# A recurrence and two layers on one core: interleaved half products, swapped rows, later conversions, and one subtraction on VectorE

## The chip, the cores and the metric

The kernel runs on one core of a Trainium2 chip. The metric is device time in microseconds (us), the median of several executions. The engines are called by the profile's names: PE (TensorE's products, PEld its weight loads), DVE (VectorE), ACT (ScalarE), POOL (GpSimd) and SP (SyncE, which issues most loads).

## The reference, cut to what matters

```python
for t in range(S):                                   # B=4, H=8, S=768, D=40
    y[:, :, t] = einsum('bhd,bhde->bhe', r_t, state)
    Sa = einsum('bhde,bhe->bhd', state, a_t)
    state = state * w_t[..., None] - einsum('bhd,bhe->bhde', Sa, b_t)
    state = state + einsum('bhd,bhe->bhde', v_t, k_t)
x = y as 3072 tokens x 320
h = x @ w_in;  x = max(h, 0)**2 @ w_out              # layer 1: 320 -> 2048 -> 320
h = x @ w_in2; out = (h - tanh(h)) @ w_out2          # layer 2
```

## The kernel before, in words

**The recurrence** is computed in six segments of 128 time steps. Two passes k cover a segment (16 of the 32 batch-heads each), so there are twelve passes, and a pass works on two halves j of eight heads. Scans on DVE (L192, L196) form the products of the decays, `front` and `keys` turn the scaled inputs on PE, `solve` inverts small triangular matrices on DVE for two passes at a time, and `back` walks through the segment in four chunks c of 32 steps. For each chunk and each half `back` multiplies the state zi by the scaled a (pu, L399, eight products of 104 rows, 32 weight columns, 40 streamed columns), ACT copies the result into rows of vu (L401), PE multiplies the keys kbn by vu (pd, L423, eight products), and DVE adds that to the state (zi, L428, two additions). In every second chunk the state is also turned (pz, L393). Half j of a chunk writes rows 64 c2 + 32 to 64 c2 + 63 of its vu, with c2 = c mod 2. `result` forms the outputs y from vu, kbn and a masked matrix (pm, am, py) and stores them for layer 1.

**The two layers** work on twelve tiles of 256 tokens each. A tile of a layer is eight steps m of 256 hidden columns: 16 products hp (L789; the fp32 values are carried as a high part xh and a low part xl), the activation, which gives gh and gl, and 12 products acc (L738) of gh and gl with the second weights wo. In layer 1 ACT makes gh and POOL makes gl (L817); the eight blocks of the second weights are loaded from DRAM anew for each tile. In layer 2 ACT runs four activations (L857 to L860), DVE forms h - tanh h (L863, and L864, L847, L848 for small h), ACT rounds it to gh (L852), and POOL subtracts gh from it (gl, L853). Ahead of each tile POOL splits its input into xh and xl (L710, L713, L714).

**The weights** arrive as 64-bit floats and are converted on the chip, piece by piece: a raw load on SP, an ACT operation, four DVE operations (L578 to L581), an ACT operation that gives the high part and a POOL subtraction for the low part (L585). Layer 1's first weights are 12 pieces of 512 columns that stay in SBUF. Its second weights are 16 pieces of 320 columns that go to DRAM, all of them before layer 1 begins. Layer 2's weights follow during layer 1, in batches of 14 pieces with a pause in front of the next solve.

**The order.** The code is written as threads (back, fronts, scalings, result, conversions, layer 1), which a planner's clock weaves together; a thread yields the time at which it may go on, and a scheduler then places the instructions of each engine by priority: `back` highest, conversions and layer 1 lowest. Each engine runs its own list in order. In the names of the rows a number behind an underscore is a buffer: zi_170 and zi_171 are the two halves' states, vu_176 and vu_177 their vu, kbn_162 and kbn_163 their keys.

## Time and profile before

| | us |
|---|---|
| median of 3 runs (lowest, highest) | 1394.27 (1388.3, 1395.91) |
| profiled execution, its own time | 1393.79 |
| its span, first to last instruction | 1391.6 |
| PE busy | 1221.7 |
| DVE busy | 947.2 |
| ACT busy | 830.0 |
| POOL busy | 675.2 |

The mean granted TensorE clock of the profiled execution is 0.941 of full speed. Layer 1's products run beside the recurrence from about 190 to 957 us; layer 2's weights are loaded after that, and layer 2's products run from about 1010 us to the end. A time of a line is the time that its engine was busy with it; it bears on the end only where the chain of waits passes through it.

### The profile page before, as it was taken

The numbers are of one execution on the slowest core, as the hardware profiler recorded it, in microseconds if no ns is written. First come the engines' busy times: TensorE is split into PE (matmuls) and PEld (weight loads), VectorE is DVE, ScalarE is ACT, GpSimd is POOL, SyncE is SP. The second block draws the span as 40 slices with busy tenths as digits, with TensorE's granted clock in tenths as the row PEclk, the third lists the DMA queues.
The fourth block names the chain that finished last, engine by engine and source line by source line (L and its number), as shares of the span: only waits on it lengthen the run. The fifth ranks groups of instructions, "written<-read, shape, count | busy, mean of one in ns | idle before, by whom it ended". The sixth has DMA issues, their size and how long they took to land.

```text
span 1391.6 us, 40716 instructions
## 1 busy us (share of the span) xinstructions
PE 1221.7 (88%) x16682; PEld 1136.5 (82%) x16682; DVE 947.2 (68%) x1812; ACT 830.0 (60%) x1768; POOL 675.2 (49%) x713
## 2 busy tenths in 40 slices
PE   1347778999799988999799999999899999999996
PEld 1246668888789877888788889999899999999995
DVE  7899785555854675356935671321269999999996
ACT  4364627574466736574465746544477777777785
POOL 5366534445444635245533643245555555555543
PEclk9986868989999988999999999999999999999999
DMA  6444544554545535454554534236920000000000
GB/s 159 114 122 143 157 150 136 154 171 137 163 138 164 170 103 161 133 157 132 160 159 134 159 103 147 85 110 217 391 72 19 24 31 22 22 22 22 22 11 22
DMA packets 94406, 164.12 MB, mean 118 GB/s; under 512 B 17696, under 2 KB 66272, under 8 KB 94212
## 3 DMA queue, kind: packets, MB, share of 16 engines
q1 hardware_dynamic: 65028, 124.02, 29.8%
q0 software_dynamic: 9600, 21.68, 5.1%
q10 hardware_dynamic: 19584, 15.74, 3.4%
q8 instruction: 134, 2.20, 0.7%
q14 instruction: 60, 0.49, 0.1%
HBM read 133.81 MB, written 27.53 MB: 116 GB/s over the span
## 4 chain that ended last, share of the span: by engine, by line
DVE 35%; PE 32%; issue 11%; ACT 10%; DMA 8%; POOL 4%; ACTq 0%; SPq 0%; POOLq 0%; DVEq 0%
DVE e L847 10%; PE hp L789 8%; PE acc L738 7%; DVE e L863 4%; DVE e L864 4%; PE pu L399 3%; DVE wx L192 3%; DMA raw<-in_moe_w_in_dram 2%; PE pd L423 2%; PE pm L451 2%; DVE inw L196 2%; PE pa L375 2%; ACT tbd L369 2%; DMA raw<-in_moe_w_out_dram 2%; DVE T L313 1%
## 5 line engine op out<-in xcount | busy, mean ns | idle before, releaser
L853 POOL TENSOR_TENSOR gl<-e,gh 128x512 fp32r<-128x512 f32 x96 | 144.3, 1504 | 180.5 <-ACT gh L852 178.3
L817 POOL TENSOR_TENSOR gl<-g,gh 128x512 fp32r<-128x512 f32 x96 | 127.0, 1323 | 177.4 <-ACT g L816 172.2
L789 PE MATMUL hp<-xh,wi 128*128 128x256 f32 x960 | 195.5, 299 | 12.3 <-ACT r L814 9.9
L789 PE MATMUL hp<-xh,wi2s 128*128 128x256 f32 x960 | 170.0, 278 | 1.7 <-DMA wi2s<-wi 1.7
L789 PEld LDWEIGHTS hp<-xh,wi 128*128 128x128 f32 x960 | 155.7, 202 | 15.7 <-ACT r L814 10.9
L847 DVE SCALAR_TENSOR_TENSOR e<-e,e 128x512 f32<-128x512 f32 x96 | 155.9, 1624 | 3.3
L738 PE MATMUL acc<-wo,gh 128*128 128x320 f32 x768 | 147.2, 327 | 3.1 <-DMA wo<-wo 2.8
L789 PEld LDWEIGHTS hp<-xh,wi2s 128*128 128x128 f32 x960 | 141.9, 188 | 1.9 <-DMA wi2s<-wi 1.9
L789 PE MATMUL hp<-xl,wi 128*128 128x256 f32 x576 | 134.9, 298 | 0.0
L738 PEld LDWEIGHTS acc<-wo,gh 128*128 128x128 f32 x768 | 121.5, 199 | 5.5 <-ACT gh L852 3.0
L428 DVE TENSOR_TENSOR zi<-pd,zi 40x160 f32<-40x160 f32 x192 | 61.8, 322 | 90.4 <-PE pd L423 86.0
L789 PE MATMUL hp<-xl,wi2s 128*128 128x256 f32 x576 | 120.7, 278 | 0.0
L852 ACT ACTIVATE gh<-e 128x512 fp32r<-128x512 f32 x96 | 60.8, 633 | 88.6 <-DVE e L848 86.4
L585 POOL TENSOR_TENSOR st<-hc,st 128x160 fp32r<-128x160 f32 (+3 forms) x72 | 51.6, 717 | 112.7 <-ACT st L584 82.3
L789 PEld LDWEIGHTS hp<-xl,wi 128*128 128x128 f32 x576 | 103.2, 203 | 0.7
L863 DVE TENSOR_TENSOR e<-hp,e 128x512 f32<-128x512 f32 x96 | 65.0, 677 | 54.4 <-ACT e L858 48.9
L476 POOL DMA_DIRECT2D yT<-yt x96 | 65.2, 682 | 71.9 <-DVE yt L475 69.7
L814 ACT ACTIVATE r<-hp 128x512 f32<-128x512 f32 x96 | 57.3, 597 | 66.7 <-PE hp L789 65.0
L789 PEld LDWEIGHTS hp<-xl,wi2s 128*128 128x128 f32 x576 | 94.5, 188 | 0.0
L578 DVE TENSOR_SCALAR hc<-hc 128x160 f32<-128x160 f32 (+3 forms) x78 | 29.2, 375 | 94.9 <-ACT hc L569 87.1
L848 DVE COPY_PREDICATED e<-e,e 128x512 f32<-128x512 int32 x96 | 89.6, 933 | 3.2
L399 PE MATMUL pu<-zi,au 104*32 104x40 f32 x1536 | 79.0, 209 | 11.1 <-DVE zi L428 8.4
(154 smaller groups left out, 3151.4 us busy)
## 6 DMA issues: line engine op xcount, KB each, us to landing
wo<-wo SPq DMA_DIRECT2D x96, 640.0 KB
inq<-in_wakb_dram SPq DMA_DIRECT2D x36, 240.0 KB
raw<-in_moe_w_in_dram SPq DMA_DIRECT2D x24, 256.0 KB
raw<-in_moe_w_out_dram SPq DMA_DIRECT2D x16, 320.0 KB
wo<-st ACTq DMA_DIRECT2D x32, 160.0 KB
wi<-st ACTq DMA_DIRECT2D x40, 128.0 KB
raw<-in_moe_w_out_dram SPq DMA_DIRECT2D x32, 160.0 KB
wo<-st ACTq DMA_DIRECT2D x64, 80.0 KB
```

Of the source, the lines that this page charges most:

```text
L399: nc.tensor.matmul(pu[r0:r0 + 32, h, :], lhsT=au[0:104, 4 * (h % 2) + h // 2, 32 * c:32 * c + 32], rhs=zi[0:104, h % 2, h // 2, :], start= ...
L428: nc.vector.tensor_tensor(out=zn, in0=pd[rows], in1=zi[rows, c2, par], op=ALU.add)
L476: getattr(nc, Q_Y).dma_start(out=self.yT[k].rearrange("(a r d) (b t) -> b r d a t", a=4, r=2, b=2)[j, par][:, :, t], in_=yt[rows])
L738: nc.tensor.matmul(acc[n][j], lhsT=g[:, i, 128 * j:128 * j + 128], rhs=w[:, p, i, :], start=(m == 0 and i == 0 and e == 0), stop=(m == 7 a ...
L789: nc.tensor.matmul(hp[:, h, :], lhsT=wt, rhs=xx, start=(e == 0), stop=(e == 7))
L814: nc.scalar.activation(out=r, in_=hp, func=ACTF.Relu)
L817: nc.gpsimd.tensor_tensor(out=gl, in0=g, in1=gh.bitcast(F32), op=ALU.subtract)
L847: nc.vector.scalar_tensor_tensor(out=u, in0=q, scalar=rest, in1=u, op0=ALU.add, op1=ALU.mult)
L848: nc.vector.copy_predicated(out=d, mask=v.bitcast(I32), data=u)
L852: nc.scalar.activation(out=gh, in_=d, func=ACTF.Copy)
L853: nc.gpsimd.tensor_tensor(out=gl, in0=d, in1=gh.bitcast(F32), op=ALU.subtract)
L863: nc.vector.tensor_tensor(out=d, in0=hp, in1=th, op=ALU.subtract)
```

## The change

Five things change.

1. In `back` both halves' pu products stand in turn, in one result tile: half 0 of the first product, half 1 of the first, half 0 of the second, and so on. Half 1 uses the other 64 rows than half 0 (64 (c2 xor j) + 32).
2. The pd products of both halves stand in turn too, in the code.
3. For half 1 the 64-row halves of vu and of the keys are swapped: vn is loaded into the swapped rows, the mask of am has a swapped second copy, and in `keys` each of the four transposes of half 1 becomes two products with the identity, of 64 weight columns each.
4. Before layer 1 only the first eight of the 16 pieces of its second weights are converted (steps 0 to 3). The other half is converted as 16 pieces of 160 columns after layer 1 has begun, before layer 2's weights, and layer 1's first tile waits with each step m from 4 on until its block is due by the planner's clock.
5. In layer 2 the subtraction that gives gl moves from POOL to DVE.

```diff
-C_LM, C_AM, C_ZERO, C_ID = 0, 32, 96, 224
+C_LM, C_AM, C_ZERO, C_ID = 0, 32, 160, 288
...
+F_W, P3, L_W1 = 4, 3, 6
...
+    c[:, C_AM + 64:C_AM + 128] = np.roll(c[:, C_AM:C_AM + 64], 64, axis=0)
...
-                nc.tensor.transpose(pt[:, pr, :], kbf[0:P, pr, blk, :], self.id[0:P, 0:P])
+                if j:
+                    for c in (0, 64):
+                        nc.tensor.matmul(pt[64 - c:128 - c, pr, :], lhsT=kbf[0:P, pr, blk, c:c + 64], rhs=self.id[0:P, 0:P], start=True, stop=True)
+                else:
+                    nc.tensor.transpose(pt[:, pr, :], kbf[0:P, pr, blk, :], self.id[0:P, 0:P])
...
-                (getattr(nc, Q_B) if k else nc.sync).dma_start(out=self.vu[j][64 * c2:64 * c2 + 32, :, :, :, 0:40], in_=vn[s, q, c2])
+                (getattr(nc, Q_B) if k else nc.sync).dma_start(out=self.vu[j][64 * (c2 ^ j):64 * (c2 ^ j) + 32, :, :, :, 0:40], in_=vn[s, q, c2])
...
-            for j in range(2):
-                q = 2 * (k % 2) + j
-                zi, vu, zt, au = self.zi[q][:, c2], self.vu[j], self.zt[j], aus[j]
-                if c2 == 0:
+            zis = [self.zi[2 * (k % 2) + j][:, c2] for j in range(2)]
+            if c2 == 0:
+                pzs = []
+                for zi in zis:
...
-                r0 = 64 * c2 + 32
-                pu = self.ps.tile([128, 8, 40], F32, tag="a", name="pu")
-                for h in range(8):
-                    nc.tensor.matmul(pu[r0:r0 + 32, h, :], lhsT=au[0:104, 4 * (h % 2) + h // 2, 32 * c:32 * c + 32],
-                                     rhs=zi[0:104, h % 2, h // 2, :], start=True, stop=True, tile_position=(0, r0))
-                nc.scalar.activation(out=vu[r0:r0 + 32, blk].rearrange("p a r d -> p (a r) d")[:, :, 0:40], in_=pu[r0:r0 + 32],
+            pu = self.ps.tile([128, 8, 40], F32, tag="a", name="pu")
+            r0 = [64 * (c2 ^ j) + 32 for j in range(2)]
+            for h in range(8):
+                for j in range(2):
+                    nc.tensor.matmul(pu[r0[j]:r0[j] + 32, h, :], lhsT=aus[j][0:104, 4 * (h % 2) + h // 2, 32 * c:32 * c + 32],
+                                     rhs=zis[j][0:104, h % 2, h // 2, :], start=True, stop=True, tile_position=(0, r0[j]))
+            clk.run(0.4)
+            for j in range(2):
+                q, vu, zt = 2 * (k % 2) + j, self.vu[j], self.zt[j]
+                nc.scalar.activation(out=vu[r0[j]:r0[j] + 32, blk].rearrange("p a r d -> p (a r) d")[:, :, 0:40], in_=pu[r0[j]:r0[j] + 32],
                                      func=ACTF.Copy, scale=-1.0)
...
+            pds = [self.ps.tile([128, 4, 40], F32, tag="a", name="pd") for _ in range(2)]
+            for pr in range(4):
+                for j, par in ((0, 0), (1, 1), (0, 1), (1, 0)):
+                    k0, hh = 64 * (c2 ^ j), 4 * par + pr
+                    nc.tensor.matmul(pds[j][64 * par:64 * par + 40, pr, :], lhsT=self.kbn[2 * (k % 2) + j][k0:k0 + 64, blk, 40 * hh:40 * hh + 40],
+                                     rhs=self.vu[j][k0:k0 + 64, blk, pr, par, 0:40], start=True, stop=True)
+            clk.run(0.5)
...
-                k0 = 64 * c2
-                pd = self.ps.tile([128, 4, 40], F32, tag="a", name="pd")
-                for pr in range(4):
-                    for par in range(2):
-                        hh = 4 * par + pr
-                        nc.tensor.matmul(pd[64 * par:64 * par + 40, pr, :], lhsT=kbn[k0:k0 + 64, blk, 40 * hh:40 * hh + 40],
-                                         rhs=vu[k0:k0 + 64, blk, pr, par, 0:40], start=True, stop=True)
...
-                                    in1=cst[:, None, C_AM:C_AM + 64].to_broadcast([128, 8, 64]), op=ALU.mult)
+                                    in1=cst[:, None, C_AM + 64 * j:C_AM + 64 * j + 64].to_broadcast([128, 8, 64]), op=ALU.mult)
...
+                yield lambda: la.wait(m)
                 w, wi = la.wo(m), la.wi(m)
...
-        nc.gpsimd.tensor_tensor(out=gl, in0=d, in1=gh.bitcast(F32), op=ALU.subtract)
+        nc.vector.tensor_tensor(out=gl, in0=d, in1=gh.bitcast(F32), op=ALU.subtract)
...
-        conv1 = cv.run([*cv.w_in(w_in1, lambda j, cols: (chunks(wi1, j, cols), lambda: None), N1), *cv.w_out(w_out1, put_out(cp1, wo1_d, N2, 2), N2)], AHEAD)
+        conv1 = cv.run([*cv.w_in(w_in1, lambda j, cols: (chunks(wi1, j, cols), lambda: None), N1), *list(cv.w_out(w_out1, put_out(cp1, wo1_d, N2, 2), N2))[:2 * F_W]], AHEAD)
+
+        wo_ready = [0] * F_W + [inf] * (8 - F_W)
...
             yield lambda: started[0]
+
+            cv = Convert(tc, l1.cp, (), nc.gpsimd, getattr(nc, Q_LD1))
+            for i, _ in enumerate(cv.run(list(cv.w_out(w_out1, put_out(l1.cp, wo1_d, DM // 2, 1), DM // 2))[4 * F_W:], 0)):
+                if i % 4 == 3:
+                    wo_ready[F_W + i // 4] = clk.t + L_W1
+                yield clk.t + P3
```

PE's list in the second pass, chunk c = 2 (pz, pu, pd of both halves; pm belongs to another pass's results), before:

```order
L393 MATMUL pz<-idt,zi_170 40x40 x8
L399 MATMUL pu<-zi_170,au 32x40 x8
L393 MATMUL pz<-idt,zi_171 40x40 x8
L399 MATMUL pu<-zi_171,au 32x40 x8
L451 MATMUL pm<-rt_178,vut 128x128 x4
L451 MATMUL pm<-rt_179,vut 128x128 x4
L423 MATMUL pd<-vu_176,kbn_162 40x40 x8
L423 MATMUL pd<-vu_177,kbn_163 40x40 x8
```

and after the change (the lines' numbers have moved: pz is L400, pu L408, pd L433):

```order
L400 MATMUL pz<-idt,zi_170 40x40 x8
L400 MATMUL pz<-idt,zi_171 40x40 x8
L408 MATMUL pu<-zi_170,au 32x40
L408 MATMUL pu<-zi_171,au 32x40
L408 MATMUL pu<-zi_170,au 32x40
L408 MATMUL pu<-zi_171,au 32x40
L408 MATMUL pu<-zi_170,au 32x40
L408 MATMUL pu<-zi_171,au 32x40
```

Eight pu of a half stood in a row; now each pu is followed by the other half's, and both pz stand ahead of them.

PE's list of the same pass, chunk c = 1 (pt of L269 are the keys' transposes, pl and pt other parts of the fronts), before:

```order
L399 MATMUL pu<-zi_170,au 32x40 x8
L250 MATMUL pl<-inq 32x64 x3
L399 MATMUL pu<-zi_171,au 32x40 x8
L250 MATMUL pl<-inq 32x64 x6
L269 MATMUL pt<-idt,inqx 128x104 x4
L250 MATMUL pl<-inq 32x64 x3
L269 MATMUL pt<-idt,inqx 128x104 x8
L423 MATMUL pd<-vu_176,kbn_162 40x40 x8
L423 MATMUL pd<-vu_177,kbn_163 40x40 x8
```

and after the change (L275 are half 0's transposes, L273 half 1's products), in the same pass one chunk earlier:

```order
L408 MATMUL pu<-zi_170,au 32x40
L408 MATMUL pu<-zi_171,au 32x40
L275 MATMUL pt<-idt,inqx 128x104 x8
L273 MATMUL pt<-idt,inqx 64x104 x8
L433 MATMUL pd<-vu_176,kbn_162 40x40 x8
L433 MATMUL pd<-vu_177,kbn_163 40x40 x8
L273 MATMUL pt<-idt,inqx 64x104 x8
```

The pd of half 0 still stand eight in a row ahead of those of half 1 here, although the code writes them in turn. Over the whole list of 768 pd, 377 follow one of the other half, 283 one of the same half and 108 another line; of 768 pu, 697 follow one of the other half and none one of the same half.

DVE's list in layer 2's middle, two steps m (e are the five buffers of the activation), before:

```order
L863 TENSOR_TENSOR e_15314<-hp_15291,e_15311 128x512
L864 TENSOR_TENSOR e_15310<-e_15310,e_15311 128x512
L847 SCALAR_TENSOR_TENSOR e_15310<-e_15313,e_15310 128x512
L848 COPY_PREDICATED e_15314<-e_15312,e_15310 128x512
L863 TENSOR_TENSOR e_15360<-hp_15337,e_15357 128x512
L864 TENSOR_TENSOR e_15356<-e_15356,e_15357 128x512
L847 SCALAR_TENSOR_TENSOR e_15356<-e_15359,e_15356 128x512
L848 COPY_PREDICATED e_15360<-e_15358,e_15356 128x512
```

and after the change (L877, L878, L861, L862 are the old L863, L864, L847, L848; L867 is gl, the old L853):

```order
L877 TENSOR_TENSOR e_15474<-hp_15451,e_15471 128x512
L878 TENSOR_TENSOR e_15470<-e_15470,e_15471 128x512
L867 TENSOR_TENSOR gl<-e_15428,gh 128x512
L861 SCALAR_TENSOR_TENSOR e_15470<-e_15473,e_15470 128x512
L862 COPY_PREDICATED e_15474<-e_15472,e_15470 128x512
L877 TENSOR_TENSOR e_15520<-hp_15497,e_15517 128x512
L878 TENSOR_TENSOR e_15516<-e_15516,e_15517 128x512
L867 TENSOR_TENSOR gl<-e_15474,gh 128x512
L861 SCALAR_TENSOR_TENSOR e_15516<-e_15519,e_15516 128x512
L862 COPY_PREDICATED e_15520<-e_15518,e_15516 128x512
```

The gl of a step stands between the next step's L878 and L861, two operations behind the L862 that completes its input.

## Rows read from the trace of the kernel before

**Rows 1.** Engines by stretch: us, busy (instructions) each, clock, DMA share, GB/s.
```profile
100.00:186.00 86.00, 66.26 (x1314) 56.33 (x1312) 71.43 (x158) 47.37 (x117) 49.32 (x51) 0.70 0.49 149
1040.00:1380.00 340.00, 332.43 (x2481) 323.20 (x2479) 328.72 (x352) 255.70 (x461) 174.42 (x118) 1.00 0.07 22
```

**Rows 2.** Output copies L878: ns min/median/max, first and last start.
```profile
L878 ACT ACTIVATE o<-accb x12: 417/424/429, 1052.5 to 1359.4; 128x320 f32<-128x320 f32 x12
```

**Rows 3.** Timeline, tile in layer 2: start, us, operation [idle <-releaser].
```profile
1172.16 1.52 POOL L853 TENSOR_TENSOR gl<-e,gh 128x512 fp32r<-128x512 f32 x1 [2.15 <-ACT gh L852]
...
1172.56 1.67 DVE L847 SCALAR_TENSOR_TENSOR e<-e,e 128x512 f32<-128x512 f32 x1
...
1174.26 0.76 DVE L848 COPY_PREDICATED e<-e,e 128x512 f32<-128x512 int32 x1
```

**Rows 4.** Timeline, layer 2's first tile, DVE and POOL.
```profile
1057.59 0.69 DVE L847 SCALAR_TENSOR_TENSOR e<-e,e 128x512 f32<-128x512 f32 x1
...
1058.32 0.78 DVE L848 COPY_PREDICATED e<-e,e 128x512 f32<-128x512 int32 x1
...
1058.98 0.67 DVE L863 TENSOR_TENSOR e<-hp,e 128x512 f32<-128x512 f32 x1
...
1059.58 0.68 DVE L864 TENSOR_TENSOR e<-e,e 128x512 f32<-128x512 f32 x1
...
1059.90 1.52 POOL L853 TENSOR_TENSOR gl<-e,gh 128x512 fp32r<-128x512 f32 x1 [2.91 <-ACT gh L852]
```

**Rows 5.** Groups, 1030 to 1380: busy us, mean ns, idle before.
```profile
L847 DVE SCALAR_TENSOR_TENSOR e<-e,e 128x512 f32<-128x512 f32 x90 | 145.6, 1618 | 3.1
...
L713 POOL TENSOR_TENSOR xl<-xraw,xh 128x512 fp32r<-128x512 f32 x10 | 17.3, 1729 | 0.1
L714 POOL TENSOR_TENSOR xl<-xraw,xh 64x256 fp32r<-64x256 f32 x10 | 12.2, 1219 | 0.0
L710 POOL CAST xh<-xraw 128x768 fp32r<-128x768 f32 x9 | 11.6, 1286 | 0.0
```

**Rows 6.** Timeline of PE in layer 2, 1147 to 1151 us.
```profile
1147.29 0.63 PE L789 MATMUL hp<-xh,wi2s 128*128 128x256 f32 x4
...
1150.96 0.28 PE L789 MATMUL hp<-xh,wi2s 128*128 128x256 f32 x1
```

**Rows 7.** Chain by line, 850 to 957 us, then 620 to 850.
```profile
by line: PE hp L789 24.0%; PE acc L738 21.4%; PE pu L399 10.7%; PE pm L451 7.6%; PE pd L423 7.4%; PE pa L375 6.6%; PE py L469 4.4%; PE pvt L443 4.2%; PE py L472 3.5%; PE pz L393 3.3%; PE pw L345 2.1%; PE pt L832 1.4%; POOL gl L817 1.2%; PE 
...
by line: issue 12.8%; PE hp L789 11.1%; PE acc L738 11.0%; PE pu L399 4.4%; DVE wx L192 4.3%; DVE inw L196 4.1%; PE pd L423 2.7%; DMA raw<-in_moe_w_out_dram 2.5%; POOL gl L817 2.5%; DVE T L313 2.5%; PE pm L451 2.1%; ACT tbd L369 2.1%; DVE t
```

**Rows 8.** Timeline of POOL at the end of the conversions before layer 1.
```profile
182.56 0.98 POOL L585 TENSOR_TENSOR st<-hc,st 128x320 fp32r<-128x320 f32 x1 [1.24 <-DMA zi<-in_vz_dram]
```

**Rows 9.** Chain of waits by line, 100 to 192 us.
```profile
by line: issue 12.7%; DVE hc L580 6.8%; PE pu L399 6.4%; DMA raw<-in_moe_w_out_dram 5.6%; PE pa L375 5.6%; ACT tbd L369 5.5%; DVE zi L428 5.1%; DVE hc L581 5.0%; DMA xraw<-yT 4.3%; DVE hc L579 3.8%; DVE hc L578 3.6%; ACTq L903 2.6%; ACT st 
```

**Rows 10.** Pieces of the chain, 394 to 442: start, us, records.
```profile
399.17 0.44 PE pz L393 x16
...
400.09 0.69 PE pu L399 x16
...
412.48 0.74 PE pd L423 x32
...
414.75 0.89 PE pm L451 x8
...
426.89 1.26 PE pu L399 x32
```

**Rows 11.** VectorE busy (x instructions) with L581 alone, by stretch.
```profile
186.00:298.00 112.00, 5.10 (x12) 0.83 0.49 147
298.00:370.00 72.00, 3.06 (x2) 0.95 0.57 164
```

**Rows 12.** Groups, whole span: busy us, mean ns, idle <-releaser.
```profile
L428 DVE TENSOR_TENSOR zi<-pd,zi 40x160 f32<-40x160 f32 x192 | 61.8, 322 | 90.4 <-PE pd L423 86.0
...
L401 ACT ACTIVATE vu<-pu 32x320 f32<-32x320 f32 x96 | 40.9, 428 | 58.2 <-PE pu L399 55.9
```

More of the change, by code (lines that the diff above doesn't have):

```diff
@@ L385, in back @@
             yield max(ready)
-            for j in range(2):
-                q = 2 * (k % 2) + j
-                zi, vu, zt, au = self.zi[q][:, c2], self.vu[j], self.zt[j], aus[j]
-                if c2 == 0:
+            zis = [self.zi[2 * (k % 2) + j][:, c2] for j in range(2)]
+            if c2 == 0:
+                pzs = []
+                for zi in zis:
                     pz = self.ps.tile([128, 4, 40], F32, tag="a", name="pz")
+                    pzs.append(pz)
                     for pr in range(4):
@@ L395, in back @@
                     clk.run(0.46)
-                r0 = 64 * c2 + 32
-                pu = self.ps.tile([128, 8, 40], F32, tag="a", name="pu")
-                for h in range(8):
-                    nc.tensor.matmul(pu[r0:r0 + 32, h, :], lhsT=au[0:104, 4 * (h % 2) + h // 2, 32 * c:32 * c + 32],
-                                     rhs=zi[0:104, h % 2, h // 2, :], start=True, stop=True, tile_position=(0, r0))
-                nc.scalar.activation(out=vu[r0:r0 + 32, blk].rearrange("p a r d -> p (a r) d")[:, :, 0:40], in_=pu[r0:r0 + 32],
-                                     func=ACTF.Copy, scale=-1.0)
+            pu = self.ps.tile([128, 8, 40], F32, tag="a", name="pu")
[8 more added lines that the diff above has]
+                nc.scalar.activation(out=vu[r0[j]:r0[j] + 32, blk].rearrange("p a r d -> p (a r) d")[:, :, 0:40], in_=pu[r0[j]:r0[j] + 32],
+                                     func=ACTF.Copy, scale=-1.0)
+                ready[j] = clk.t + L_E
+                if c2:
+                    self.u_ready[k][j][blk] = ready[j]
+            for j in range(2):
+                q, zt = 2 * (k % 2) + j, self.zt[j]
                 if c2 == 0:
                     for p0 in (0, 64):
-                        nc.scalar.activation(out=zt[p0:p0 + 40, blk], in_=pz[p0:p0 + 40].rearrange("p a d -> p (a d)"), func=ACTF.Copy)
+                        nc.scalar.activation(out=zt[p0:p0 + 40, blk], in_=pzs[j][p0:p0 + 40].rearrange("p a d -> p (a d)"), func=ACTF.Copy)
                 if c < 2:
@@ L409, in back @@
                     self.v_load(s + 1, q, c - 2)
-                clk.run(0.28)
-                ready[j] = clk.t + L_E
-                if c2:
-                    self.u_ready[k][j][blk] = ready[j]
             yield max(ready)
+            pds = [self.ps.tile([128, 4, 40], F32, tag="a", name="pd") for _ in range(2)]
[5 more added lines that the diff above has]
+            clk.run(0.5)
             for j in range(2):
                 q = 2 * (k % 2) + j
-                vu, kbn, zi, wx = self.vu[j], self.kbn[q], self.zi[q], self.wx[2 * (k and (k - 1) % 3 + 1) + j]
-                k0 = 64 * c2
-                pd = self.ps.tile([128, 4, 40], F32, tag="a", name="pd")
-                for pr in range(4):
-                    for par in range(2):
-                        hh = 4 * par + pr
-                        nc.tensor.matmul(pd[64 * par:64 * par + 40, pr, :], lhsT=kbn[k0:k0 + 64, blk, 40 * hh:40 * hh + 40],
-                                         rhs=vu[k0:k0 + 64, blk, pr, par, 0:40], start=True, stop=True)
+                zi, wx, pd = self.zi[q], self.wx[2 * (k and (k - 1) % 3 + 1) + j], pds[j]
                 for par in range(2):
@@ L430, in back @@
                         nc.vector.tensor_tensor(out=zn, in0=zn, in1=wx[rows, :, 128:129].to_broadcast([40, 4, 40]), op=ALU.mult)
-                clk.run(0.4)
                 ready[j] = clk.t + L_E
@@ L717, in attn_moe, with __init__ @@
     class Layer:
-        def __init__(self, mo, load, hpool, accs, wi, wo, act, done, depth, flush=lambda mo: None, ahead=5, ready=lambda k: 0):
+        def __init__(self, mo, load, hpool, accs, wi, wo, act, done, depth, flush=lambda mo: None, ahead=5, ready=lambda k: 0, wait=lambda m: 0):
             self.mo, self.load, self.hpool, self.accs, self.wi, self.wo = mo, load, hpool, accs, wi, wo
-            self.act, self.done, self.depth, self.flush, self.ahead, self.ready = act, done, depth, flush, ahead, ready
+            self.act, self.done, self.depth, self.flush, self.ahead, self.ready, self.wait = act, done, depth, flush, ahead, ready, wait
     clk, now = Clock(), [None]
@@ L1004, in acc2 @@
             return accs[n % 2]
-        l1 = Layer(None, lambda k: load_cols(l1.mo, yT[k]), h_tile, lambda n: acc0, lambda m: wi1[:, m], wo1, act1, done1, 1, ready=lambda k: A.y_ready[k])
+        l1 = Layer(None, lambda k: load_cols(l1.mo, yT[k]), h_tile, lambda n: acc0, lambda m: wi1[:, m], wo1, act1, done1, 1, ready=lambda k: A.y_ready[k], wait=lambda m: wo_ready[m])
         l2 = Layer(None, lambda k: load_cols(l1.mo, x1T[k]), lambda: ps_a.tile([128, 2, 256], F32, tag="a", name="hp2"),
```

## The prediction

> **What bounds the kernel now.** I read the engines by stretch first. In the start, shown from 100 to 186 us, DVE carries most, 71.4 of 86 us, and TensorE's granted clock is 0.70, a mean of its two levels [rows 1]. In layer 2, from 1040 to 1380 us, PE is busy 332 and DVE 329 of 340 us at the full clock [rows 1]. What lies between is attention together with layer 1 (to 957 us), then the loading of layer 2's weights; for the former I read the chain of waits, below.
>
> Layer 2. Its output copies give the pace: the first tile's stands at 1052.5 us, the eleventh tile's second one at 1359.4, a copy takes 0.42, so ten tiles in 306.5 us, 30.65 us each [rows 2]. A tile is eight steps m, and in a step DVE runs L863, L864, L847, L848. From L847 to L848 it is 1.70 us where L847 starts beside POOL's L853 [rows 3], and 0.73 where L847 starts with POOL idle; the others follow each other by 0.66 (L848 to L863), 0.60 (L863 to L864), and L864's 0.68 with the gap of 0.04 that stands behind L847 is 0.72 [rows 4]. A step of DVE is therefore 0.60 + 0.72 + 1.70 + 0.66 = 3.68 us. Over layer 2 the mean of L847 is 1618 ns against 0.69 undisturbed, so almost every one is held up [rows 4, 5]. PE needs the same time: a step's products hp start at 1147.29, the next step's at 1150.96, 3.67 us apart [rows 6]. So DVE and PE both ask for 29.4 us a tile, and the other 1.25 I put down to POOL's three operations that split the next tile (L710, L713, L714 [rows 5]), which stop DVE once more.
>
> Attention and layer 1. From 850 to 957 us the lines that make up the chain are nearly all PE's; from 620 to 850 issue holds 12.8%, two lines of the scans (L192, L196) 8.4%, and PE's first two lines only 22% [rows 7]. What PE spends is worth its full price in that last tenth of the attention, and about half before it.
>
> The start. Layer 1 begins when the converted second weights are stored; POOL finishes the last piece of them at 183.5 us [rows 8]. Conversion lines (L578 to L581, 19.2%) and raw loads of those weights (5.6%) are 24.8% of the chain from 100 to 192 us, 22.8 us [rows 9].
>
> **Part 1, the two halves' u-products in turn (L399).** In the chain 16 records of pu take 0.69 us, and two halves back to back 1.26; 16 records of pz, with the same 104 rows and 40 streamed columns, but alternating between two column groups, take 0.44 [rows 10]. A product of these is two records, eight products are 16; the second record of a product has to follow the first on the same columns of the array, and what alternates can lie over it. 32 alternating records of such a kind are in the trace as pd x32, 0.74 us [rows 10]. In the new order pu alternates throughout. So a chunk saves 1.26 or twice 0.69, less 0.74: 0.52 to 0.64, and 48 chunks 25 to 31; I take 28.
> A rule speaks against that: the Trainium skill, TensorE: Matmul & The Clock Gate, section Part 3 (Packing small matmuls), says that weight loads lie over running products only where the row groups differ. Both halves' pu use rows 0 to 103, so by it nothing would be saved, and the sum below would be 15 us higher; pz has equal rows too, and its 0.44 against 0.69 says otherwise.
>
> **Part 2, the d-products in turn (L423), rows swapped.** What is written is that four quarters of the array work in turn. But pd already alternates columns inside a half (0.74 for 32 [rows 10]), and the new order of the engine puts the eight of one half and then the eight of the other in a row at many places, as the change section shows. I count a gain of 0 to 0.12 a chunk (a sixth of 0.74), 0 to 6 us, and take 2.
>
> **Part 3, the price of the swap (L269).** For half 1 four transposes become eight products of two records, each over 104 columns. Eight product records of 128 columns take 0.89 us (pm) [rows 10], 0.11 each, so 0.09 at 104 columns. Four transposes of one record then cost 0.36; 16 records cost 1.44 one after the other, 0.77 if each second one is covered, as in pz (half of 1.44, and 0.05 for the start). There are 24 such groups: +10 (covered) to +26 us. They alternate columns like pz, so I take 10. The other mask and the swapped target of the vu loads add no instruction.
>
> PE therefore gives up 28 + 2 - 10 = 20 us. A sixth of it (the last two of twelve passes, 3.3 us) lies where PE alone is the chain; of the rest I count 45%, 7.5 us. **-11 us**, ends -25 (all of it, and the upper saving) and 0.
>
> **Part 4, half the conversions moved behind the start of layer 1.** Eight pieces go, of the 28 of layer 1's weights (12 of the first, 16 of the second). If the 22.8 us [rows 9] belonged to all 28 alike, eight would be 6.5 us; if only to the 16, 11.4. **-8**, ends -15 (eight of twelve that lie in the stretch) and 0 (the chain goes on through u-products and DVE). They come back as 16 pieces of half the width, before the first layer-2 pieces. Those stood in batches with a pause in front of the next solve: L581 runs 12 times in 186 to 298 us and 2 times in 298 to 370 [rows 11]. The moved pieces push the first batch into that pause, where scans and the solve of the next pair lie: at most six pieces of four DVE operations of 0.43 us (5.10 over 12), 0 to 10 us; **+4**. On SP (the queue of the loads) the new loads of wo's steps 4 to 7 stand behind the raw loads of their own pieces; behind them wait zi and inq loads, whose slack I take as enough.
>
> **Part 5, layer 2's gl from POOL to DVE (L853).** DVE's step becomes 0.60 + 0.72 + 0.72 for gl (like L864 it has two SBUF inputs of 128x512) + 0.73 for L847 undisturbed + 0.66 [rows 4]: 3.43, 27.4 us a tile. To this come POOL's three operations: 1.25 (what a tile loses now) to 4.2 us (their own 1.73 + 1.22 + 1.29 [rows 5]), so 28.7 to 31.6 against PE's 29.4. Gl waits for ACT's gh, issued behind four activations of the next step; ACT is busy 256 of 340 us [rows 1], and two DVE operations (1.3 us) lie between L848 and gl, so I add no wait. POOL's operations lose the DVE operation that they met, and I stay near what a tile loses now: PE decides, 29.45. That is 1.2 us for ten tiles, and 2 us for the first tile, where L847 is held up alike. **-14**, ends -20 and +10 (31.6 a tile).
>
> **The sum.** -11 - 8 + 4 - 14 = -29 us on the profiled execution's 1393.8 (span 1391.6): **1365 us**. The median of the runs shown, 1394.3, is the same within 0.5 us.
>
> **Rivals.**
> (a) The chunk's chain gets longer. Pu of half 0 now stands behind the zi adds of half 1 (two of 322 ns), and pd, where it alternates, behind both vu copies (428 ns more [rows 12]): 1.07 us on 48 chunks, +51, no PE gain: 1394 + 51 - 4 - 14 = 1427. It decides from 0.6 us a chunk (29/48) on. For it: DVE's zi adds wait 86 us for pd [rows 12]. Against it: PE has other lines to run between a chunk's steps, in both stretches hp and acc lead PE's lines [rows 7].
> (b) POOL's three operations stop DVE in layer 2 for much of their time: at 3.25 us a tile (27.4 + 3.25 = 30.65) layer 2 gains nothing, 1379; at all of 4.2 it is 1389.
> (c) Pu does not overlap, its equal rows stand against it and pz's pace has another cause: PE gets +8 instead of -20, +4 on the path: 1394 + 4 - 4 - 14 = 1380. The rule cited under part 1 is this case.
> (d) Attention waits on scans and solves whatever PE does: the -11 falls away, 1376.
> (e) The change does not do what it says, products and pieces staying in their old order in time: excluded for pu, which alternates in the engine's list.
>
> **How the numbers follow.** Forecast 0.60, (a) 0.07, (b) 0.13, (c) 0.08, (d) 0.12. From the ends, -25 - 15 + 0 - 20 gives 1334 as the low end; (c), (d) and most of (b) lie below 1388, which is the high end. 0.5% (7 us) is about what a measurement of this kernel can tell from no change: below 1387 lie the forecast, (d) and most of (b) and (c), 0.86; within 0.5% I put 0.07, for the upper end of (b) and two of these together; slower 0.07, (a).
>
> **What would show it.** Layer 2: L847 near 0.69 us, a tile at 29.4 to 29.7 us, PE without idle time. Pu: 32 records in about 0.75 us, pd unchanged. L269's half-1 groups at 0.8 us. Layer 1's first hp about 8 us earlier. The forecast is wrong if chunks get longer in spite of shorter pu, if PE waits for wo in the first tile of layer 1, or if DVE holds 30.5 us a tile.

## The result, and the profile after

The changed kernel takes 1347.4 us (median of four runs, 1345.7 to 1349.5) beside 1391.3 us for the kernel before. The ratio is 0.9692, with a 95% interval of 0.9638 to 0.9747, so 43 us less (35 to 50). The forecast was 1365, 29 us less, with a range of 1334 to 1388. The profiled execution has a span of 1344.6 us, 47 less than before's 1391.6.

Four events cut the two profiled executions into stretches:

| event | before, us | after, us | gained up to it | forecast |
|---|---|---|---|---|
| layer 1's first hp | 192.3 | 184.0 | 8.3 | 8 |
| the last yT (end of the recurrence) | 953.1 | 936.9 | 16.2 | 15 |
| layer 2's first output copy | 1052.5 | 1027.5 | 25.0 | 17 |
| layer 2's last output copy | 1383.5 | 1337.6 | 45.9 | 29 |

The starts of the first products hp (before) and of the stores of yT (before and after) come from these lines:

```profile
L789 PE MATMUL hp<-xh,wi x960: 274/283/583, 192.3 to 1015.3; 128*128 128x256 f32 x192
L476 POOL DMA_DIRECT2D yT<-yt x96: 646/674/920, 137.2 to 953.1; - x96
```

```profile
L489 POOL DMA_DIRECT2D yT<-yt x96: 646/674/922, 140.5 to 936.9; - x96
```

Up to the last yT the sum seems to hold to a microsecond. That is luck: the experiments show that two of its terms are far off there and nearly cancel.

**Layer 2.** After the change the output copies (duration min/median/max in ns, first and last start) are:

```profile
L892 ACT ACTIVATE o<-accb x12: 434/437/448, 1027.5 to 1314.4; 128x320 f32<-128x320 f32 x12
```

Against [rows 2] ten tiles take 1314.4 - 0.44 - 1027.5 = 286.5 us, 28.65 each, where they took 30.65. The engines by stretch (us of PE, PEld, DVE, ACT, POOL, then clock, DMA share, GB/s), to be set beside [rows 1]:

```profile
100.00:186.00 86.00, 63.74 (x1350) 54.14 (x1350) 67.91 (x175) 40.36 (x100) 44.19 (x47) 0.67 0.40 123
1000.00:1330.00 330.00, 329.25 (x2570) 329.05 (x2569) 305.73 (x452) 265.27 (x479) 38.42 (x34) 1.00 0.08 25
```

POOL has fallen from 174 of 340 us to 38 of 330, and PE now stands at 329 of 330. DVE's step in the middle of a tile (start us, us):

```profile
1137.59 0.69 DVE L861 SCALAR_TENSOR_TENSOR e<-e,e 128x512 f32<-128x512 f32 x1
1138.31 0.78 DVE L862 COPY_PREDICATED e<-e,e 128x512 f32<-128x512 int32 x1
1138.99 0.67 DVE L877 TENSOR_TENSOR e<-hp,e 128x512 f32<-128x512 f32 x1
1139.58 0.67 DVE L878 TENSOR_TENSOR e<-e,e 128x512 f32<-128x512 f32 x1
1140.18 0.68 DVE L867 TENSOR_TENSOR gl<-e,gh 128x512 fp32r<-128x512 f32 x1
1140.78 0.68 DVE L861 SCALAR_TENSOR_TENSOR e<-e,e 128x512 f32<-128x512 f32 x1
```

From L878 to L878 on DVE there are five operations now, and none is held up: L867 (the moved gl) 0.60 us after L878, L861 0.60 after that, L862 0.72, L877 0.68, L878 0.59, a step of 3.19 us where [rows 3, 4] gave 3.68 and I worked out 3.43 (I gave gl and the operation ahead of it 0.72 us each; they take 0.60). The groups in 1005 to 1330 us (busy us, mean ns, idle before):

```profile
L861 DVE SCALAR_TENSOR_TENSOR e<-e,e 128x512 f32<-128x512 f32 x90 | 67.9, 755 | 0.5
...
L878 DVE TENSOR_TENSOR e<-e,e 128x512 f32<-128x512 f32 x89 | 61.8, 694 | 16.3 <-ACT e L874 16.3
```

L861's mean is 755 ns (L847 had 1618 in [rows 5]), and DVE waits 16.3 us for ACT at L878. DVE has slack, and PE, busy for 329 of 330 us, is the bound.

**The chunk's products.** Pieces of the chain, the counterparts of [rows 10]:

```profile
413.88 0.74 PE pz L400 x32
414.62 0.70 PE pu L408 x32
...
418.62 0.45 PE pd L433 x32
```

Both halves' pu, 32 records, take 0.70 us (1.26 before), and both halves' pd 0.45 (0.74 before) where they stand in turn. The groups over the whole span, before (busy us, mean ns, idle before):

```profile
L399 PE MATMUL pu<-zi,au 104*32 104x40 f32 x1536 | 79.0, 209 | 11.1 <-DVE zi L428 8.4 <-ACT lc L253 1.0 <-ACT zt L405 0.6
...
L423 PE MATMUL pd<-vu,kbn 64*40 64x40 f32 x1536 | 55.2, 211 | 4.2 <-DVE rhs L254 3.1 <-ACT vu L401 1.1
...
L269 PE MATMUL pt<-idt,inq 104*128 104x104 f32 x160 | 22.6, 277 | 2.8 <-DVE yt L475 2.7 <-ACT kbn L271 0.2
...
L269 PE MATMUL pt<-idt,inqx 104*128 104x104 f32 x32 | 5.4, 326 | 1.1 <-DVE rhs L254 0.8 <-ACT kbn L271 0.3
```

and after (L408 is pu, L433 pd, L275 and L273 the keys of half 0 and half 1):

```profile
L433 PE MATMUL pd<-vu,kbn 64*40 64x40 f32 x1536 | 50.0, 218 | 9.7 <-ACT vu L413 8.6 <-DVE rhs L256 0.9 <-issue 0.2
L408 PE MATMUL pu<-zi,au 104*32 104x40 f32 x1536 | 48.7, 214 | 16.0 <-DVE zi L442 10.1 <-issue 4.3 <-ACT st L597 1.3
...
L273 PE MATMUL pt<-idt,inq 104*64 104x104 f32 x320 | 19.9, 265 | 2.0 <-DVE yt L488 2.0
...
L275 PE MATMUL pt<-idt,inq 104*128 104x104 f32 x80 | 10.5, 271 | 2.0 <-ACT kbn L277 2.0
...
L273 PE MATMUL pt<-idt,inqx 104*64 104x104 f32 x64 | 5.0, 323 | 0.3 <-DVE yt L488 0.3
...
L275 PE MATMUL pt<-idt,inqx 104*128 104x104 f32 x16 | 2.6, 325 | 0.7 <-DVE rhs L256 0.7
```

Pu goes from 79.0 to 48.7 us, pd from 55.2 to 50.0, the keys from 28.0 to 38.0.

**The start.** Layer 1's first hp (the starts stand behind the durations):

```profile
L803 PE MATMUL hp<-xh,wi x960: 275/283/583, 184.0 to 994.3; 128*128 128x256 f32 x192
```

It starts at 184.0 us; it was 192.3.

### The profile page after: what moved, and what is told of

It is laid out like the page before. It is cut to its first block, busy times and chain, and to the rows that moved or that the text cites. A ratio compares the mean times of both kernels' runs of the same rounds, so it can differ in the third digit from the quotient of the medians.

```text
span 1344.6 us, 41226 instructions
## 1 busy us (share of the span) xinstructions
PE 1186.5 (88%) x16970; PEld 1113.0 (83%) x16970; DVE 918.3 (68%) x1942; ACT 834.2 (62%) x1784; POOL 525.4 (39%) x623
## 4 chain that ended last, share of the span: by engine, by line
PE 54%; DVE 22%; ACT 8%; DMA 7%; issue 6%; POOL 1%; SPq 0%; ACTq 0%; DVEq 0%; POOLq 0%
PE hp L803 19%; PE acc L751 13%; PE accb L751 6%; DVE wx L194 3%; DVE T L319 2%; PE pu L408 2%; DVE inw L198 2%; PE pa L381 2%; DMA raw<-in_moe_w_in_dram 2%; ACT tbd L375 2%; PE pd L433 2%; DVE tt L315 2%; DVE hc L594 2%; PE pm L464 2%; DVE hc L593 2%
## 5 line engine op out<-in xcount | busy, mean ns | idle before, releaser
L831 POOL TENSOR_TENSOR gl<-g,gh 128x512 fp32r<-128x512 f32 x96 | 128.1, 1334 | 171.3 <-ACT g L830 157.2
L803 PE MATMUL hp<-xh,wi2s 128*128 128x256 f32 x960 | 167.3, 277 | 1.6 <-POOL xh L723 1.6
L723 POOL CAST xh<-xraw 128x768 fp32r<-128x768 f32 x24 | 21.2, 882 | 255.4 <-PE hp L803 238.4
L591 DVE TENSOR_SCALAR hc<-hc 128x160 f32<-128x160 f32 (+3 forms) x88 | 33.4, 381 | 105.0 <-ACT hc L582 76.2
L877 DVE TENSOR_TENSOR e<-hp,e 128x512 f32<-128x512 f32 x96 | 65.2, 679 | 43.3 <-ACT e L872 43.2
L862 DVE COPY_PREDICATED e<-e,e 128x512 f32<-128x512 int32 x96 | 86.2, 897 | 2.8
L871 ACT ACTIVATE e<-hp 128x512 f32<-128x512 f32 x96 | 57.2, 596 | 49.5 <-PE hp L803 45.1
L489 POOL DMA_DIRECT2D yT<-yt x96 | 65.0, 680 | 46.4 <-DVE yt L488 45.7
L381 PE MATMUL pa<-tbd,rhs 128*104 128x128 f32 x384 | 56.0, 307 | 28.5 <-ACT tbd L375 27.6
L878 DVE TENSOR_TENSOR e<-e,e 128x512 f32<-128x512 f32 x96 | 67.1, 699 | 19.1 <-ACT e L874 19.1
```

The costliest lines, as they stand in the source:

```text
L381: nc.tensor.matmul(pa[0:104, i, :], lhsT=self.rhs[q][:, i, 40 * g:40 * g + 104], rhs=self.tbd[:, 4 * g + i, :], start=True, stop=True)
L489: getattr(nc, Q_Y).dma_start(out=self.yT[k].rearrange("(a r d) (b t) -> b r d a t", a=4, r=2, b=2)[j, par][:, :, t], in_=yt[rows])
L803: nc.tensor.matmul(hp[:, h, :], lhsT=wt, rhs=xx, start=(e == 0), stop=(e == 7))
L831: nc.gpsimd.tensor_tensor(out=gl, in0=g, in1=gh.bitcast(F32), op=ALU.subtract)
L862: nc.vector.copy_predicated(out=d, mask=v.bitcast(I32), data=u)
L871: nc.scalar.activation(out=s, in_=hp, func=ACTF.Square)
```

## The experiments

All ratios are to the kernel before, measured beside it on the same chip. The intervals are some 0.004 to 0.008 to either side. A difference between two of these kernels is therefore uncertain by about 10 us to either side, and differences of a few us say nothing.

**1. Layer 2's gl alone.** The kernel before with one line changed:

```diff
-        nc.gpsimd.tensor_tensor(out=gl, in0=d, in1=gh.bitcast(F32), op=ALU.subtract)
+        nc.vector.tensor_tensor(out=gl, in0=d, in1=gh.bitcast(F32), op=ALU.subtract)
```

> The kernel before with one edit: layer 2's gl on VectorE. Theory A (the gain of layer 2 is the gl move alone, with the quicker pace of PE's hp products that the trace of after shows, 113 ns from product to product against 117): a tile 28.6 us, the first tile's end 9 us earlier relative to the last yT, together -30 us, ratio 0.978 to 0.980. Theory B (the quicker pace of hp comes from another part, such as where the buffers lie): hp stays at 117 ns, PE's step at 3.67 us, a tile at 29.4 us, -14 to -18 us, ratio 0.988 to 0.990.

Measured: 0.9872 (0.9832 to 0.9912), 18 us less. Its output copies:

```profile
L878 ACT ACTIVATE o<-accb x12: 434/438/447, 1051.7 to 1345.0; 128x320 f32<-128x320 f32 x12
```

A tile is (1345.0 - 0.44 - 1051.7) / 10 = 29.29 us. The tile and the total are theory B's. The gain lies almost wholly behind the first output copy: in the profiled execution that copy stands at 1051.7 us, 0.8 earlier than before, and from it to the end of the span it takes 324.0 us, against 339.1. From the last yT to the first output copy it takes 90.2 us, against 99.3, but here the last yT stands 8.4 us later than before (961.5 for 953.1), so these 9 us can't be booked as a gain.

**2. The changed kernel with gl back on POOL**, the same line the other way round.

> The changed kernel with layer 2's gl back on GpSimd. Theory A: a tile at 30.65 us again, hp at 117 ns, ratio to the kernel before 0.989 to 0.992 (what parts 1 to 4 give alone, -11 to -16 us). Theory B: hp stays at 113 ns, a tile below 30.2 us, ratio 0.980 to 0.985.

Measured: 0.9884 (0.9827 to 0.9940), 26 us above the changed kernel. Its copies:

```profile
L892 ACT ACTIVATE o<-accb x12: 417/424/432, 1028.4 to 1335.5; 128x320 f32<-128x320 f32 x12
```

That is 30.67 us a tile, as before the change. From the last yT to the first output copy it takes 94.4 us here and 90.6 in the changed kernel. So the move of gl is worth 18 to 26 us, and parts 1 to 4 together 16 (8 to 24).

**3. The pace of hp.** In the profiled execution of the changed kernel 16 products hp take from 1131.22 to 1133.04, 1.82 us (0.1138 each):

```profile
1131.22 0.62 PE L803 MATMUL hp<-xh,wi2s 128*128 128x256 f32 x4
...
1133.04 0.46 PE L751 MATMUL accb<-wo2s,gh 128*128 128x320 f32 x2
```

> The changed kernel once more, beside the next three on one chip. Theory A (the split of the conversions costs more than the start gains): ratio 0.968 to 0.972, and so 10 us or more above the kernels without the split. Rival (the gap of no_split to the changed kernel was a difference between chips): ratio 0.957 to 0.962. For the pace of hp in layer 2: if it is a state that the code sets, 113 ns again; if it is a state that an execution falls into, either 113 or 117.

Measured: 0.9700 (0.9637 to 0.9763), the same kernel as above. But in this execution the 16 products take 1139.12 to 1141.00, 1.88 us (0.1175 each):

```profile
1139.12 0.63 PE L803 MATMUL hp<-xh,wi2s 128*128 128x256 f32 x4
...
1141.00 0.61 PE L751 MATMUL acc<-wo2s,gh 128*128 128x320 f32 x3
```

and a tile (1311.8 - 0.44 - 1018.5) / 10 = 29.29 us:

```profile
L892 ACT ACTIVATE o<-accb x12: 432/438/448, 1018.5 to 1311.8; 128x320 f32<-128x320 f32 x12
```

So the quicker pace is no part of the change: the same program ran through the last ten tiles of layer 2 at one pace in one execution and at the other in the next. Between the two lie 0.64 us a tile, 7 us in eleven tiles.

**4. No split of the conversions.** The changed kernel with all of layer 1's second weights converted ahead, as before:

```diff
-F_W, P3, L_W1 = 4, 3, 6
+F_W, P3, L_W1 = 8, 3, 6
```

> The changed kernel with all 16 pieces of layer 1's second weights converted before layer 1, as in the kernel before. Theory A (the split gains what the start loses, and gives part of it back between 350 and 660 us): layer 1's first hp at about 192 us, the solves of 502 and 662 us no later than now, the end 2 to 6 us later than the changed kernel, ratio 0.971 to 0.974. Rival: the moved pieces cost in the middle as much as the start gains, the end is the same, ratio 0.968 to 0.970.

Measured: 0.9585 (0.9509 to 0.9662), 15 us below the changed kernel. That was so far from both expectations that it was run again with more rounds.

> no_split once more, with more rounds. Theory A (the split costs about 15 us of what the other parts give): ratio 0.955 to 0.962, clearly below the changed kernel's 0.969 and 0.970. Rival (the first measurement of no_split was low by chance, its variants at 0.970 to 0.974 are the rule): ratio 0.965 to 0.971, and the split costs nothing that can be measured. In its trace the stretch from layer 1's first hp to the last yT holds 50 to 60 us of idle PE, as in all the others.

Measured: 0.9577 (0.9533 to 0.9621), median 1329.6 us. The interval lies wholly below the changed kernel's. Beside the other four parts, part 4 therefore costs some 16 us, although it does start layer 1 earlier (184.0 instead of 193.6 and 192.1 us). This is the fastest version of this study, 59 us below the kernel before. The cost isn't the same in every version: with pu in blocks (run 6) the kernel with the split and the one without it can't be told apart.

One place where the two kernels differ: conversions on DVE, ACT and POOL in the 30 us ahead of a solve and during it. The changed kernel, solves of 335.6 and 501.9 us (busy us and instructions of DVE, ACT, POOL on the tile hc, then clock, DMA share, GB/s):

```profile
305.60:356.00 50.40, 11.37 (x24) 5.91 (x13) 4.49 (x6) 0.97 0.71 209
471.90:521.40 49.50, 9.00 (x24) 5.42 (x12) 4.23 (x6) 0.97 0.63 191
```

Without the split, solves of 337.3 and 489.3 us:

```profile
307.30:356.70 49.40, 0.00 (x0) 0.00 (x0) 0.00 (x0) 0.93 0.42 128
459.30:505.90 46.60, 4.74 (x10) 1.89 (x5) 2.11 (x3) 0.96 0.56 169
```

With the split 24 DVE operations stand there each time, 9 to 11 us together; without it none and 10. Between the end of the last zi of one pass and the start of the first pw of the pass that needs the solve lie 24.7, 22.7, 21.0, 22.3 us in the kernel before, 26.6, 24.4, 24.3, 23.1 in the changed one, and 22.0, 20.7, 20.9, 20.6 without the split: 14 us more in four pauses with it.

**5. Batches held clear of the solves.** The changed kernel, the first batch of layer 2's pieces cut from 14 to 6, so that it ends where a batch ended:

```diff
-            begun = [0]
+            begun = [8]
```

> The changed kernel (with the split); of layer 2's weights the first batch before a solve is 6 pieces instead of 14, so that the moved pieces and it together are as much as a batch was; the last 8 pieces wait for the last solve. Theory A (the split costs because each batch of layer 2's pieces now runs into the next solve and the scans ahead of it): the pauses between passes 3 and 4, 5 and 6, 7 and 8 fall from 24 to 27 us to about 21, the start's 9 us stay, the end is 10 to 20 us earlier than the changed kernel, ratio 0.955 to 0.963. Rival (layer 1's early start itself fills PE and the queues and delays the attention): pauses stay above 24 us, ratio 0.967 to 0.972.

Measured: 0.9689 (0.9631 to 0.9747), no gain. The conversions did leave most of the place (solves of 329.8 and 485.2 us):

```profile
299.80:347.30 47.50, 9.16 (x16) 3.80 (x8) 2.90 (x4) 1.00 0.67 204
455.20:503.10 47.90, 4.79 (x6) 1.34 (x3) 1.92 (x2) 0.94 0.52 157
```

and the pauses fell to 23.8, 20.7, 20.7, 20.5 us, 13 less together. But the time from a pass's first pw to its first pu grew from 31.1 to 32.6 us on the mean, 18 us over twelve passes. So theory A was right about the pauses and wrong about the end. That the pieces taken out of the pauses come back elsewhere is a reading, not shown; what in the moved pieces makes the attention longer is not settled.

**6. The products in turn or in blocks.** The changed kernel with the loops over h and j exchanged, first with the split:

```diff
-            for h in range(8):
-                for j in range(2):
+            for j in range(2):
+                for h in range(8):
```

> The changed kernel with the eight pu products of half 0 ahead of those of half 1, all else (swapped rows, one result tile) as it is. Theory A (products in turn lie over each other): 32 pu take 1.26 us instead of 0.70, PE's busy time rises by 22 to 27 us, and 45% of it reaches the end: 10 us, ratio 0.975 to 0.978. Rival (attention waits on other engines whatever PE does): busy time rises as much, the end moves under 3 us, ratio 0.969 to 0.971. Rival (no overlap): pu's time does not change.

Measured: 0.9724 (0.9668 to 0.9779), 3 to 4 us above the changed kernel, inside the noise. Then the same without the split:

> no_split with the eight pu of half 0 ahead of those of half 1. Theory A (PE's saved time reaches the end once the conversions don't stand in the way): 15 to 25 us above no_split, ratio 0.970 to 0.977. Rival (the rest of back's new order, such as both pz and both vu copies together, gives the gain): within 5 us of no_split, ratio 0.957 to 0.962.

Measured: 0.9738 (0.9683 to 0.9794), 22 us above no_split. Pu in blocks and in turn, both without the split:

```profile
L408 PE MATMUL pu<-zi,au 104*32 104x40 f32 x1536 | 68.5, 216 | 10.7 <-issue 5.2 <-ACT au L383 2.7 <-ACT st L597 2.2
```

```profile
L408 PE MATMUL pu<-zi,au 104*32 104x40 f32 x1536 | 47.0, 212 | 11.9 <-ACT au L383 4.0 <-DVE zi L442 3.9 <-issue 2.1
```

That is 21.5 us of pu on PE, and 22 us (12 to 32) at the end. With the split pu in blocks takes

```profile
L408 PE MATMUL pu<-zi,au 104*32 104x40 f32 x1536 | 66.7, 211 | 7.9 <-DVE zi L442 6.1 <-DVE rhs L256 0.9 <-ACT rhs L243 0.5
```

against 48.7 us in turn, 18.0 us on PE and 4 us (-7 to 15) at the end: PE's busy time was the same in both orders there (1185.8 us in blocks, 1186.5 in turn), since its other products were shorter by what pu was longer; no run gives the reason for that. So what the same order of products is worth at the end isn't one number: by these two pairs anything from nothing to the full price, 13 us in the mean.

**7. In turn, but without the swapped rows.** no_split with both halves' pu on the same 32 columns of the array:

```diff
-            r0 = [64 * (c2 ^ j) + 32 for j in range(2)]
+            r0 = [64 * c2 + 32 for j in range(2)]
...
-                if j:
+                if 0:
...
-                    k0, hh = 64 * (c2 ^ j), 4 * par + pr
+                    k0, hh = 64 * c2, 4 * par + pr
```

(with it a pu tile for each half, vn's rows and the mask as in the kernel before).

> no_split without the swapped rows: both halves' pu in turn, but on the same 32 columns of the array, in a result tile each; half 1's keys by four transposes again, one mask. Theory A (only products on different columns lie over each other): 32 pu in a row take 1.26 us again, PE gets 22 us for pu and gives back 10 at the keys, so 5 to 12 us above no_split, ratio 0.962 to 0.968. Rival (turns between the halves are enough, whatever the columns): 32 pu at 0.7 us, PE 10 us less busy than no_split, ratio 0.950 to 0.957.

Measured: 0.9696 (0.9631 to 0.9760), 16 us above no_split. Pu is where it was before the change:

```profile
L408 PE MATMUL pu<-zi,au 104*32 104x40 f32 x1536 | 78.7, 214 | 9.6 <-DVE zi L442 5.6 <-ACT au L383 1.9 <-ACT lc L255 1.0
```

78.7 us, against 79.0 in the kernel before and 47.0 with the swap. Turns alone give nothing; it is the other columns that let two products lie over each other, with the same 104 rows in both. The pd products say the same; without the swap, then with it:

```profile
L433 PE MATMUL pd<-vu,kbn 64*40 64x40 f32 x1536 | 57.4, 214 | 6.7 <-ACT vu L413 6.6
```

```profile
L433 PE MATMUL pd<-vu,kbn 64*40 64x40 f32 x1536 | 45.7, 213 | 11.8 <-ACT vu L413 8.9 <-issue 1.5 <-DVE rhs L256 0.9
```

The result tiles of pu differ between these two kernels as well (one for each half here, one for both with the swap). They can't be the reason for pd, which has a tile for each half in both. The rule of the Trainium skill that was weighed under part 1 (TensorE: Matmul & The Clock Gate, Part 3) speaks of weight loads; that it leaves nothing to save here was the prediction's inference from it. With that inference the trace does not agree: 47.0 us stand against 78.7, with equal rows.

**8. The attention's parts alone**, without the split and with gl on POOL.

> The attention's parts alone: no split of the conversions, layer 2's gl on GpSimd, swapped rows and products in turn. Theory A (parts add up: all of no_split's 0.9585 less gl_alone's 0.9872): -35 to -40 us, ratio 0.970 to 0.975. Rival (no_split gained through the order of its pieces, not through the products): -11 us as predicted for parts 1 to 3, ratio 0.990 to 0.993. Layer 2's tile 30.7 us either way.

Measured: 0.9725 (0.9653 to 0.9797), 38 us less than the kernel before (28 to 48), more than three times the 11 that I gave parts 1 to 3. The parts add up: 38 here and 18 for gl are 56, and no_split measured 59.

**9. The planner's costs.** `back` tells the planner shorter times for a chunk's products (0.4 and 0.5 us for both halves instead of 0.56 and 0.8). First no_split with the old ones:

```diff
-            clk.run(0.4)
+            clk.run(0.56)
...
-            clk.run(0.5)
+            clk.run(0.8)
```

> no_split with the planner's old costs for a chunk of both halves (0.56 and 0.8 us instead of 0.4 and 0.5); the products and their order within back are those of no_split. Theory A (the chunk got shorter because both halves' products stand together, with nothing of layer 1 between them): a chunk's period stays near 9.1 us, ratio within 0.005 of no_split, 0.954 to 0.963. Rival (the planner weaves other work differently since it believes chunks to be shorter): a chunk's period of 9.6 us or more, ratio 0.965 to 0.975.

Measured: 0.9725 (0.9669 to 0.9782), 20 us above no_split, although a chunk (from its first pu to the next chunk's, the mean of the 36 such distances in the trace) takes 8.7 us, no longer than no_split's 9.1. What is longer is the way to a pass's first chunk: from its first pw to its first pu it takes 33.9 us on the mean, against 30.9 in no_split. Then the kernel with gl alone and the new costs (0.2 and 0.25 a half):

> gl_alone (the kernel before with layer 2's gl on VectorE) with the planner's costs for a chunk lowered to those of the changed kernel (0.2 and 0.25 us a half), products and order in the code as before. Theory A (the order of the products, not the planner's numbers, shortens the chunk): a chunk's period stays at about 10.2 us, ratio within 0.005 of gl_alone's 0.987. Rival (the planner's numbers do it): a chunk's period of 9.5 us or less, ratio 0.965 to 0.975.

Measured: 0.9844 (0.9789 to 0.9899), against 0.9872 for gl alone: no difference that can be told, and a chunk of 10.3 us as with the old costs. So the new order in `back` shortens the chunk, from 10.2 to 9.1 us, whatever the planner believes. Most of that is not the overlap of the products: with pu in blocks, and without the swap, a chunk takes 9.4 us. With the new order the planner's numbers move the end by 20 us (10 to 31), by themselves they move nothing that can be told, and the new order with the old numbers gives 20 (11 to 30) against gl alone.

These new costs are a sixth change. They stand in the diff (`clk.run(0.4)`, `clk.run(0.5)`), but not in the list of five.

Set side by side, the runs show a limit of the whole comparison. no_split stands at 0.958. With any one thing taken out of it or added to it, the end comes to nearly the same place: the split 0.969 and 0.970, no swap 0.970, the old costs 0.9725, pu in blocks 0.974. Two at once (the split and pu in blocks) give 0.9724, no more than one. Costs that added up would not do that (gl's gain does add up, by run 8). A rival is left that no run excludes: each edit makes the planner weave all the threads anew, and no_split's weave is a good one that each of these edits loses. It is no chance of one measurement (0.9585 and 0.9577), but which part of a difference is the edit's own cost and which the new weave's isn't separated.

**What the stretch from layer 1's first hp to the last yT shows.** PE's busy us (instructions), clock, DMA share, GB/s, in the kernel before:

```profile
192.30:953.10 760.80, 705.28 (x11512) 0.94 0.48 141
```

the changed kernel, and its second execution:

```profile
184.00:936.90 752.90, 694.93 (x11781) 0.91 0.50 149
```

```profile
182.80:928.50 745.70, 685.15 (x11780) 0.93 0.50 150
```

no_split (second execution):

```profile
192.10:916.00 723.90, 668.95 (x11780) 0.94 0.48 147
```

pu in blocks and no swap, both without the split:

```profile
197.00:947.10 750.10, 687.95 (x11795) 0.93 0.47 142
```

```profile
191.80:936.00 744.20, 694.36 (x11555) 0.93 0.48 143
```

pu in blocks with the split, and no_split with the planner's old costs:

```profile
183.20:935.90 752.70, 685.10 (x11769) 0.94 0.50 149
```

```profile
192.30:942.40 750.10, 690.26 (x11782) 0.93 0.46 142
```

The length less PE's busy time is 55.5, 58.0, 60.6, 54.9, 62.1, 49.8, 67.6 and 59.8 us, in the same order. The length varies by 37 us, PE's idle time by 18. Layer 1 is a store of work that PE can take up when the recurrence waits, and most of the difference in length is PE's busy time. But that busy time is not fixed by the products alone. With the planner's old costs the same products as no_split's keep PE busy for 690.3 us instead of 669.0 (678.8 in no_split's first execution), pd 55.3 us over the whole span instead of 45.7: the weave bears on it too. And with pu in blocks beside the split PE was idle for 67.6 us, 7 to 10 more than in the changed kernel's two executions.

## Why the prediction held, and where it did not

The sign was right and the measured 1347 us lie in the range, 18 below the forecast. That the sum came so close is luck: two wrong terms nearly cancelled. Attention gave 38 us instead of 11, and the split took 16 instead of giving 4. With gl's 18 that is 40, and 43 were measured.

- **Part 1, size.** Right. 28 us of pu forecast, 30.3 measured (79.0 to 48.7); 32 records at 0.74 forecast, 0.70 measured. The mechanism, other columns and equal rows, was told apart by run 7. Rival (c) is out.
- **Part 2.** Right within its ends, 2 forecast, 5.2 measured. Where pd does stand in turn the gain is 0.29 us a chunk (0.74 to 0.45), not the 0.12 that I set as the most: four quarters do overlap. I judged that from pd's pace inside a half, and the row had two columns in turn, not two rows as well. So the sign that I gave, pd unchanged, did not come.
- **Part 3.** Right: +10 forecast, 28.0 to 38.0 measured.
- **What parts 1 to 3 give at the end.** This step failed: 11 us forecast, 38 (28 to 48) measured in run 8, more than all of the 25 us that PE's products gave up (30.3 + 5.2 - 10.0). I had put the planner's new costs for a chunk at nothing, without a reason. With the old ones about 20 of the 38 us are left (run 9). The 45% of PE's gain that I priced, by the share of PE's lines in the chain of waits [rows 7], is not settled either way: about 20 us (11 to 30) at the end for PE's 25 lie above my 11 without excluding it, and the two pairs of run 6 give 22 us for 21.5 and 4 for 18. So no run supports one fixed share. I should have read the busy time of the stretch, 705 of 761 us, beside the chain: most of the versions' difference is in that busy time.
- **The chunk's order.** I had rival (a), a longer chunk, and no case for a shorter one. The chunk's distance fell from 10.2 to 9.1 us. A likely reason is that the two halves' products and copies stand together: from a chunk's first pu to the end of its last it takes 3.3 us on the mean before, 1.3 in the changed kernel, and 1.5 with pu in blocks. That is argued, not tested. A shorter chunk alone doesn't make the end earlier, since the run with the shortest, 8.7 us, ends 20 us after no_split. How much of the 38 us comes from the chunk and how much from PE's products was not separated.
- **Part 4.** The start's 8 us are right (8.3 measured). The give-back was priced as one batch pushed into one pause, 0 to 10 us, and taken as 4. Against no_split it is 24 (16 of loss and 8 of gain). All four pauses are longer with the split, not one; that it is the pauses alone was refuted by run 5, and why the split costs nothing beside pu in blocks is open.
- **Part 5.** Right in size and in its place: the tile was forecast at 29.45 and is 29.29 in gl_alone and in the second execution of the changed kernel; 18 us (12 to 23) measured for 14, and 15 of the 16 us between the two profiled executions lie behind the first output copy. What the first tile gives is not well known: the first output copy comes 0.8 us earlier in gl_alone than before and 0.9 earlier in the changed kernel than in run 2, and from the last yT to it the time falls by 9.1 and 3.8 us; 2 were forecast. One cause there I had not named. In the kernel before, POOL's list holds layer 1's gl (L817) behind layer 2's L853, and that waits for ACT (start us, us, and in brackets the wait):

```profile
998.52 1.29 POOL L853 TENSOR_TENSOR gl<-e,gh 128x512 fp32r<-128x512 f32 x1 [3.38 <-ACT gh L852]
...
1000.88 1.30 POOL L817 TENSOR_TENSOR gl<-g,gh 128x512 fp32r<-128x512 f32 x1
1004.24 1.30 POOL L853 TENSOR_TENSOR gl<-e,gh 128x512 fp32r<-128x512 f32 x1 [2.06 <-ACT gh L852]
...
1005.61 1.26 POOL L817 TENSOR_TENSOR gl<-g,gh 128x512 fp32r<-128x512 f32 x1
```

  With gl on DVE these waits of POOL, 3.4 and 2.1 us, are gone, and layer 1's last tile no longer stands behind them. I had named what is queued behind gl on DVE, and not what had been queued behind it on POOL. What these waits cost at the end isn't shown.
- **The 0.64 us a tile that I did not forecast**, 28.65 instead of 29.29 in the profiled execution, is the pace of hp, which the same kernel has in one execution and not in another (run 3). It is 7 of the 47 us between the two profiled spans and no effect of the change.
- Rival (b) is out: POOL's operations still meet DVE once a tile, but DVE has 0.4 us of slack in each step. Rivals (a) and (d) are out by run 8.

## What to carry to other kernels

Where one engine has a store of independent work, read its busy and idle time in the stretch beside its share of the chain of waits, and don't price a saving on it by one fixed share: here 21.5 us of products were 22 us at the end in one pair of kernels, and 18 were 4 in another. Where a planner places the work, its cost numbers are part of the change and need a run of their own: here they moved the end by 20 us. When an operation leaves an engine, look at what stood behind it in that engine's list as well as at what will stand behind it in the new one. And work that is moved out of a start into a stretch that is already woven tight has to be tried without the move: here the move gave 8 us and took 24.
